# Score pairs put ahead of a block: an earlier third pair, fewer copied pairs, and two more blocks that begin ahead

## The chip, the core and the metric

The kernel runs on one core of a Trainium2 chip. The core has a matrix engine (TensorE, in the profile PE for matmuls and PEld for weight loads), three engines for elementwise work (VectorE = DVE, ScalarE = ACT, GpSimd = POOL), SyncE (SP), which issues most transfers, and 16 DMA engines. Every engine takes its own instructions in order and waits on semaphores for the others. Matmuls write to PSUM banks, from which VectorE and ScalarE read. The metric is the time of one execution on the device in microseconds; the median over the runs is compared.

## The reference

One block of a transformer, batch 1, 2048 tokens of 512 features, float32:

```python
x = A_x
xn = _layernorm(x, axis=-1)
s = _A_ref(xn, A_wqkv, A_wo)                      # softmax attention, 32 heads of 16, then @ wo
g = _silu(_B_ref(xn, B_w_gate, B_w_up, B_w_down)) # (silu(xn@w_gate) * (xn@w_up)) @ w_down, 1792 wide
return x + s * g
```

Attention is over all 2048 x 2048 pairs of every head, with a softmax scale of 16^-0.5.

## The kernel before

**Prologue** (the first exponential of the attention starts at 157.0 us): the layer norm, the transposes of the normalised tokens, and the projections to queries, keys and values, in four token blocks of 512. Each block has twelve tiles of output. A table `COPIES` says behind which of these tiles ScalarE copies pieces of the transposed tokens into `fx`, from which the feed-forward network reads later (16 pieces, 1.05 us each). In the same stretch ScalarE casts the transposed tokens of the next block into `xt` (L649), VectorE makes the residual of that cast (L652), and TensorE needs both at the next block's first tile. Projected tiles land in four PSUM buffers `ps`.

**Attention** then runs in 32 units (8 groups of 4 heads x 4 query blocks of 512), each over 16 key tiles of 128. A unit is cut into three blocks of 4 to 6 key tiles, which gives 96 blocks, numbered 0 to 95 by `now`. In a block of n key tiles there are 2n *pairs*: a pair is the scores of one key tile for two heads, two matmuls that use the upper and the lower half of the array's rows, 128 x 1024 numbers in all. A pair is turned to probabilities in one of two ways:

- *direct* (event D): both matmuls go into one of the two score tiles (two banks each), and ScalarE exponentiates straight from there into a pair buffer `pr` (L948). The two tiles alternate, so a pair's matmuls wait until the exponential of the pair two before it is done;
- *copied* (events A and B): the two halves go one after the other through one spare bank (`acc1`, in the order below `acc_81`), VectorE copies each to the pair buffer (L1005 and L1011), and ScalarE exponentiates it in place at the block's end (L1019).

Between these, TensorE works on the other branch: event F is one *product step*, two matmuls into `bankx` and `banky`, of the feed-forward network (L187) or, in the last nine blocks, of the output projection (L378). These D, A, B and F make up the block's *mixed part*. Behind it come the *values* (L407): the products of probabilities and values for the block's key tiles, four column tiles of the array at once, eight matmul records for each key tile, accumulated in `acc0`. There are 12 pair buffers.

What sets the order is a planner, `events(n, f)`: for a block of n key tiles and f product steps it decides how many pairs are copied, gives every D, A and B a mark on an abstract time line on which a product step and a direct pair are one unit, and fills the rest with F. The first two D are at marks 0 and 1, the next at 7, then one every `gap` units.

**The tail.** From block 87 (`early`) on, the product steps come from the output projection, and some blocks *begin ahead*: `run` leaves the last key tile's values of the block before, first scores two pairs of the next block (`begin`), and then does those last values. The exponentials of these two pairs can so run while TensorE ends the values. Before the change this holds for blocks 87, 88 and 89. The blocks from 87 have (n, f) = (6, 18), (5, 12), (5, 12), (6, 24), (6, 24), (4, 12), (4, 12), (6, 24), (6, 24).

The output projection splits each group of products in two halves, between which the two banks change row halves: before the second half TensorE waits for two one-element copies on VectorE, `turned_over` (L382), and behind the second VectorE takes the result from the banks (`closing`: L200 into `facc`, L361 with the gate). In block 87 this turn lies within the mixed part, after 9 of 18 steps; in 88 and 92 it falls at the block's end, since each has one half of a group. VectorE's other work (`chores`: transposes of finished units L418 and L443, residuals of the projection's operands L327, L453 and L1017) is put between the copies where the planner sees room, and the closing reads wait until the last copy of the block has been issued. GpSimd adds the result to x and stores it (L362, L363).

Of the kernel before, what the change touches and what calls it, by code (L numbers as in the profile page):

```python
# [21 lines left out]
D = 512  # L22
# [5 lines left out]
NT = TB // P  # L28
# [14 lines left out]
PROBS = 12  # L43
EPS = 1e-5
TURNS = (0, 0, 0, 0, 0, 2, 4, 6, 8, 10, 13, 16, 16)
COPIES = ((0, 0, 0, 1, 1, 1, 1, 0, 0, 0, 1, 1), (1, 1, 0, 0, 1, 1, 1, 1, 2, 2, 0, 0))
QSLOT = (0, 1, 0)
KSLOT = (0, 0, 1)

# [2 lines left out]
def tile_block(ctx: ExitStack, tc: tile.TileContext, x, wqkv, wo, w_gate, w_up, w_down, out):  # L52
# [87 lines left out]
    def tidy(room=None):  # L140
        while chores and (room is None or chores[0][0] <= room):
            cost, work = chores.pop(0)
            work()
            if room is not None:
                room -= cost
# [19 lines left out]
    def catch_up():  # L165
        while after:
            after.pop(0)()
# [30 lines left out]
    def close():  # L198
        while closing:
            closing.pop(0)()  # L200
# [136 lines left out]
    def out_steps():  # L337
        if now == early:
            for c in range(DT - 1):
                load_out(0, c)  # L340
        if now == early + 1:
            for c in range(DT - 1):
                load_out(1, c)
            for t in range(NT):
                load_gates(t)
        if now == early + 2:
            for c in range(DT - 1):
                load_out(2, c)
        if now == opened[units - 1] + 1:
            load_gate()  # L350

    def out_splits():
        for b, c in {early: ((0, 0), (0, 1), (0, 2)), early + 2: ((1, 0), (1, 1)), early + 3: ((1, 2),),
                     early + 5: ((2, 0), (2, 1)), early + 6: ((2, 2),)}.get(now, ()):
            split_out(b, c)
        if now == len(blocks) - 1:
            for j in range(EARLY):
                gate_rest(j)
# [109 lines left out]
    now = -1  # L468

    def fill(n):  # L470
        nonlocal given
        while n > 0 and queue:
            next(queue[0][0])
            queue[0][1] -= 1
            if not queue[0][1]:
                queue.pop(0)
            n -= 1
            given += 1
# [7 lines left out]
    early = len(sizes)  # L486
# [16 lines left out]
            blocks.append((u, kt, n))  # L503
            kt += n

    def events(n, f):
        length = 2 * n + f
        need = 2 * n - max(2, (10 * length + 46) // 40)
        fit = (10 * length + 55) // 112
        copied = max(0, min(need, fit)) if now else 0  # L510
        direct = 2 * n - copied
        gap = max(4, min(5, (length - 8) / max(1, direct - 2)))
        marks = [(0, "D"), (1, "D")] + [(7 + gap * i, "D") for i in range(direct - 2)]
        marks += [(2.2 + max(5.6, min(8, (length - 5) / (2 * copied))) * i, "AB"[i % 2]) for i in range(2 * copied)]
        marks.sort(key=lambda mark: mark[0] - 0.6 * (mark[1] == "D"))
        out = []
        at = left = 0
        for t, kind in marks:
            while left < f - (kind != "D") and at < t:
                out.append((at, "F"))  # L520
                left += 1
                at += 1
            out.append((at, kind))
            at += 1 if kind == "D" else 0.5
        return direct, out + [(at + i, "F") for i in range(f - left)]

    with ExitStack() as pro:
# [119 lines left out]
        def split_x(b, t, av, between=None):  # L647
            hi, lo = (xt[b % 2][j][:, :, t * P:(t + 1) * P] for j in range(2))
            nc.scalar.copy(hi, av)  # L649
            if between:  # L650
                between()
            dve.tensor_sub(lo, av, hi.bitcast(F32))  # L652
# [119 lines left out]
        def copy_fx(i):  # L772
            i, w = divmod(i, 2)
            i, u = divmod(i, 2)
            j, h = divmod(i, 2)
            dst = fx[halves[h], j].rearrange("p (c u) t -> u p c t", u=2)[u]
            nc.scalar.copy(dst[:, 2 * w:2 * w + 2], xt[0][j][halves[u], 2 * w:2 * w + 2])

        copied = list(range(16))
# [11 lines left out]
        for b in range(NB):  # L791
# [3 lines left out]
            for n, (make, i) in enumerate(slots):  # L795
# [27 lines left out]
                if b == 0 and n == 2:  # L823
                    split_x(0, 0, xf)
                for _ in range(COPIES[b][n] if b < 2 else 0):
                    copy_fx(copied.pop(0))
# [108 lines left out]
    now = 0  # L935
# [3 lines left out]
    def scores(u, bank, kt, j, h):  # L939
        k, kc = kst[(u // NB * NB + kt // CT) % RING], kt % CT  # L940
        r = slice(h * HALF, h * HALF + NROW)
        mm(bank, k[r, j, kc * P:(kc + 1) * P], qst[u % 2][r, j], start=True, stop=True)  # L942

    def scored(u, slot, kt, j):
        for h in order():
            scores(u, score[slot][:, h], kt, j, h)
        pr = ppool.tile([P, 2, TB], F32, tag="pr", name="pr")
        act(pr, score[slot], AF.Exp, scale=0.25)  # L948
        return pr

    begun = {}

    def begin(u, first, n):
        for j in range(2):
            begun[first, j] = scored(u, j, first, j)

    def run(u, first, n):
        nonlocal lower
        f = sizes.pop(0) if sizes else 0
        direct, todo = events(n, f)  # L960
        if now == 0:
            for _ in range(4):
                todo.insert(0, todo.pop(max(i for i, (_, e) in enumerate(todo) if e == "F")))
        if now >= early and f != pair // 2:
            behind = [i for i, (_, e) in enumerate(todo) if e == "F"][f // 2]
            near = min((i for i, (_, e) in enumerate(todo) if e == "D"), key=lambda i: abs(i - behind))
            todo.insert(behind - (near < behind), todo.pop(near))
        pairs = [(kt, j) for kt in range(first, first + n) for j in range(2)]
        straight, copies = pairs[:direct], pairs[direct:]
        probs, waiting, turned_in = {}, [], []  # L970

        def unit_end():
            while ends:
                ends.pop(0)()
            out_steps()

        done = len(begun)
        if done:
            probs.update(begun)
            begun.clear()  # L980
            todo = [i for i in todo if i not in ((0, "D"), (1, "D"))]
            unit_end()
        copying = [t + 1.5 for t, e in todo if e in "AB"]
        final = max(at for at, (_, e) in enumerate(todo) if e == "F")
        free = 0
        for at, (t, e) in enumerate(todo):
            if at == final and not copying:
                tidy()
            if e == "F":
                fill(1)  # L990
            elif e == "D":
                probs[straight[done]] = scored(u, done % 2, *straight[done])
                done += 1
                if done == 2:
                    unit_end()
            elif e == "A":
                if now > early and not turned_in:
                    turned_in.append(now)
                    out_splits()
                kt, j = copies.pop(0)  # L1000
                waiting.append((kt, j))
                scores(u, spare_bank, kt, j, 0)
                lower = True
                probs[kt, j] = ppool.tile([P, 2, TB], F32, tag="pr", name="pr")
                dve.tensor_copy(probs[kt, j][:, 0], spare_bank)  # L1005
                free = copying.pop(0) + 3
            else:
                kt, j = waiting[-1]
                scores(u, spare_bank, kt, j, 1)
                lower = False  # L1010
                dve.tensor_copy(probs[kt, j][:, 1], spare_bank)  # L1011
                free = copying.pop(0) + 3
            if not copying:
                close()
            while chores and at < final and (not copying or max(free, t) + chores[0][0] <= copying[0] + 0.5):
                free = max(free, t) + chores[0][0]
                chores.pop(0)[1]()  # L1017
        for kt, j in waiting:
            act(probs[kt, j], probs[kt, j], AF.Exp, scale=0.25)  # L1019
        tidy()  # L1020
        if not turned_in:
            out_splits()
            tidy()
        catch_up()
        kts = range(first, first + n)
        if early <= now + 1 < early + NT - 1:
            values(u, kts[:-1], probs)
            begin(*blocks[now + 1])
            values(u, kts[-1:], probs)
        else:  # L1030
            values(u, kts, probs)
# [104 lines left out]
```

## Time and profile before

| what | value |
|---|---|
| median of 3 runs (lowest to highest) | 1399.99 us (1399.34 to 1401.33) |
| profiled execution: time, span | 1399.14 us, 1397.4 us |
| TensorE clock granted in the profile | 1.0 |
| ScalarE exponentials from scores (L948) | 857, 1032 ns mean |
| ScalarE exponentials of copied pairs (L1019) | 167, 1080 ns mean |
| VectorE copies of half pairs (L1005, L1011) | 167 each, 692 and 691 ns mean |

A row of a timeline gives the start in us from the span's start, the length in us (from the first start to the last end where rows are merged), engine, line, operation, output<-inputs and shapes, how many were merged, and in brackets the idle time before it with what ended it. A row of the chain of waits gives the start, the time that the chain spent there, and engine, tile and line; it is followed back from the last instruction, and TensorE's marks in it lie 0.07 us behind the starts of the timeline. Matmuls overlap, two row halves and one after the other, so starts and not lengths show TensorE's pace.

### The profile page before, as it was taken

The numbers are of one execution on the slowest core, as the hardware profiler recorded it, in microseconds if no ns is written. First come the engines' busy times: TensorE is split into PE (matmuls) and PEld (weight loads), VectorE is DVE, ScalarE is ACT, GpSimd is POOL, SyncE is SP. The second block draws the span as 40 slices with busy tenths as digits, with TensorE's granted clock in tenths as the row PEclk, the third lists the DMA queues.
The fourth block names the chain that finished last, engine by engine and source line by source line (L and its number), as shares of the span: only waits on it lengthen the run. The fifth ranks groups of instructions, "written<-read, shape, count | busy, mean of one in ns | idle before, by whom it ended". The sixth has DMA issues, their size and how long they took to land.

```text
span 1397.4 us, 27647 instructions
## 1 busy us (share of the span) xinstructions
PE 1388.9 (99%) x11193; PEld 848.9 (61%) x11193; DVE 763.1 (55%) x1299; ACT 1087.9 (78%) x1245; POOL 73.9 (5%) x92
## 2 busy tenths in 40 slices
PE   9999999999999999999999999999999999999998
PEld 7777755655665665566556556655655665565555
DVE  6674555455645653556456635554565446556454
ACT  6753678877888877787888778778877887888885
POOL 4200200000000000000000000000000000000222
PEclk9999999999999999999999999999999999999999
DMA  7778741043634411254514303356224113225323
GB/s 228 270 244 266 181 102 43 13 116 84 133 85 118 118 43 36 54 134 92 139 51 110 94 13 73 76 145 145 63 73 112 35 47 73 66 88 163 99 74 142
DMA packets 126953, 148.13 MB, mean 106 GB/s; under 512 B 12524, under 2 KB 79340, under 8 KB 126052
## 3 DMA queue, kind: packets, MB, share of 16 engines
q1 hardware_dynamic: 121620, 125.79, 35.3%
q0 software_dynamic: 4912, 20.12, 3.8%
q8 instruction: 89, 1.46, 0.5%
q14 instruction: 44, 0.36, 0.1%
q10 hardware_dynamic: 288, 0.39, 0.1%
HBM read 106.68 MB, written 39.58 MB: 105 GB/s over the span
## 4 chain that ended last, share of the span: by engine, by line
PE 87%; ACT 1%; issue 0%; DVE 0%; DVEq 0%; ACTq 0%
PE acc L407 32%; PE bankx L187 23%; PE score L942 16%; PE banky L187 9%; PE acc L942 3%; PE bankx L378 1%; PE banky L378 1%; ACT pr L948 1%; PE acc L1073 0%; PE bankx L1073 0%; PE score L1073 0%; DVE pr L1005 0%; DVE y L1080 0%; DVE y L1086 0%; DVEq L1132 0%
## 5 line engine op out<-in xcount | busy, mean ns | idle before, releaser
L948 ACT ACTIVATE pr<-score 128x1024 f32<-128x1024 f32 x857 | 810.3, 1032 | 227.8 <-PE score L942 226.3
L407 PE MATMUL acc<-pr,vst 128*17 128x512 f32 x4096 | 459.7, 593 | 0.0
L942 PE MATMUL score<-qst,kst 50*128 50x512 f32 x1714 | 393.8, 413 | 1.5 <-ACT pr L948 1.4
L187 PE MATMUL bankx<-fx,guh 64*128 64x512 f32 x896 | 333.2, 393 | 0.1
L187 PE MATMUL banky<-fx,guh 64*128 64x512 f32 x896 | 324.6, 393 | 0.0
L407 PEld LDWEIGHTS acc<-pr,vst 128*17 128x17 f32 x4096 | 110.4, 97 | 291.6 <-issue 269.9
L942 PEld LDWEIGHTS score<-qst,kst 50*128 50x128 f32 x1714 | 174.6, 184 | 147.0 <-issue 73.1
L1005 DVE COPY pr<-acc 128x512 f32<-128x512 f32 x167 | 115.5, 692 | 191.6 <-PE acc L942 187.5
L187 PE MATMUL bankx<-wd,hh 64*128 64x512 f32 x672 | 199.9, 392 | 0.0
L187 PE MATMUL banky<-wd,hh 64*128 64x512 f32 x672 | 197.7, 393 | 0.0
L187 PEld LDWEIGHTS bankx<-fx,guh 64*128 64x128 f32 x896 | 166.4, 186 | 18.5 <-issue 0.9
L187 PE MATMUL banky<-fx,gul 64*128 64x512 f32 x448 | 175.5, 392 | 0.0
L187 PE MATMUL bankx<-fx,gul 64*128 64x512 f32 x448 | 175.2, 391 | 0.0
L1019 ACT ACTIVATE pr<-pr 128x1024 f32<-128x1024 f32 x167 | 171.2, 1080 | 0.0
L187 PEld LDWEIGHTS banky<-fx,guh 64*128 64x128 f32 x896 | 166.4, 186 | 5.1
L1011 DVE COPY pr<-acc 128x512 f32<-128x512 f32 x167 | 115.4, 691 | 74.3 <-PE acc L942 63.4
L240 DVE SCALAR_TENSOR_TENSOR ga<-th,bankx 128x512 f32<-128x512 f32 x56 | 38.5, 688 | 178.4 <-ACT th L239 178.4
L942 PE MATMUL acc<-qst,kst 50*128 50x512 f32 x334 | 134.2, 402 | 0.1
L187 PEld LDWEIGHTS bankx<-wd,hh 64*128 64x128 f32 x672 | 125.0, 186 | 12.9
L187 PEld LDWEIGHTS banky<-wd,hh 64*128 64x128 f32 x672 | 124.5, 186 | 3.3
L187 PEld LDWEIGHTS bankx<-fx,gul 64*128 64x128 f32 x448 | 83.6, 187 | 10.4
L187 PEld LDWEIGHTS banky<-fx,gul 64*128 64x128 f32 x448 | 83.5, 186 | 2.5
(184 smaller groups left out, 1298.2 us busy)
## 6 DMA issues: line engine op xcount, KB each, us to landing
gur<-in_B_w_gate_dram SPq DMA_DIRECT2D x56, 256.0 KB
gur<-in_B_w_up_dram SPq DMA_DIRECT2D x56, 256.0 KB
wdr<-in_B_w_down_dram SPq DMA_DIRECT2D x56, 256.0 KB
kst<-k_d SPq DMA_DIRECT2D x192, 64.0 KB
qst<-q_d SPq DMA_DIRECT2D x192, 64.0 KB
fx<-xt_d SPq DMA_DIRECT2D x24, 512.0 KB
q_d<-parts SPq DMA_DIRECT2D x16, 512.0 KB
k_d<-parts SPq DMA_DIRECT2D x16, 512.0 KB
```

The costliest lines, as they stand in the source:

```text
L187: mm(banks[i], lhs[halves[i]], rhs[halves[i]], start=start, stop=stop)
L240: dve.scalar_tensor_tensor(ga, th, 1.0, bankx, op0=ALU.add, op1=ALU.mult)
L378: mm(banks[k], lhs[b, c][a][halves[h], (j + k) * P:(j + k + 1) * P], fx[halves[h], w, c], start=swap == i == 0, stop=i == 3 * n - 1, skip_ ...
L407: mm(acc[0][h * 32:h * 32 + DH + 1], v[:, kt % CT, h * (DH + 1):(h + 1) * (DH + 1)], probs[kt, h // 2][:, h % 2], start=kt == 0, stop=kt = ...
L942: mm(bank, k[r, j, kc * P:(kc + 1) * P], qst[u % 2][r, j], start=True, stop=True)
L948: act(pr, score[slot], AF.Exp, scale=0.25)
L1005: dve.tensor_copy(probs[kt, j][:, 0], spare_bank)
L1011: dve.tensor_copy(probs[kt, j][:, 1], spare_bank)
L1019: act(probs[kt, j], probs[kt, j], AF.Exp, scale=0.25)
```

## The change

Three edits:

1. `events` is told how many pairs were put ahead (`ahead`, 0 or 2). With 2 it doesn't plan the first two D, counts the block as two units shorter, marks the third pair at 0.5 instead of 7 and the first half copy at 0.3 instead of 2.2, and copies n - 3 pairs. For n = 6 and n = 5 that is as many as before (3 and 2), for n = 4 it is 1 instead of 2. The line in `run` that took the first two D out afterwards goes.
2. The blocks that begin ahead are 87, 88, 89 and now also 92 and 93, the two blocks of 4 key tiles.
3. In the first prologue block, the `fx` copy that stood behind the eleventh tile goes behind the twelfth, beside the one there.

```diff
-COPIES = ((0, 0, 0, 1, 1, 1, 1, 0, 0, 0, 1, 1), (1, 1, 0, 0, 1, 1, 1, 1, 2, 2, 0, 0))
+COPIES = ((0, 0, 0, 1, 1, 1, 1, 0, 0, 0, 0, 2), (1, 1, 0, 0, 1, 1, 1, 1, 2, 2, 0, 0))
...
-    def events(n, f):
-        length = 2 * n + f
+    def events(n, f, ahead):
+        length = 2 * n - ahead + f
         need = 2 * n - max(2, (10 * length + 46) // 40)
         fit = (10 * length + 55) // 112
-        copied = max(0, min(need, fit)) if now else 0
+        copied = n - 3 if ahead else max(0, min(need, fit)) if now else 0
         direct = 2 * n - copied
         gap = max(4, min(5, (length - 8) / max(1, direct - 2)))
-        marks = [(0, "D"), (1, "D")] + [(7 + gap * i, "D") for i in range(direct - 2)]
-        marks += [(2.2 + max(5.6, min(8, (length - 5) / (2 * copied))) * i, "AB"[i % 2]) for i in range(2 * copied)]
+        marks = [] if ahead else [(0, "D"), (1, "D")]
+        marks += [((0.5 if ahead else 7) + gap * i, "D") for i in range(direct - 2)]
+        marks += [((0.3 if ahead else 2.2) + max(5.6, min(8, (length - 5) / (2 * copied))) * i, "AB"[i % 2]) for i in range(2 * copied)]
...
-        direct, todo = events(n, f)
+        direct, todo = events(n, f, len(begun))
...
-            todo = [i for i in todo if i not in ((0, "D"), (1, "D"))]
...
-        if early <= now + 1 < early + NT - 1:
+        if now + 1 - early in (0, 1, 2, 5, 6):
```

The number of pair buffers (12) stays. Lines between `events` and the removed line in `run` stand one lower in the changed kernel: L942 becomes L943, L948 becomes L949; L1005, L1011 and L1019 stay.

On VectorE, at the start of block 87, before (`acc_81` is the spare bank, `acc_80` holds the values of the unit that ended, `wor` and `fx` are the last output weights being split):

```order
L1017 CAST fx<-wor 128x512
L1005 COPY pr<-acc_81 128x512
L1017 TENSOR_TENSOR fx<-wor,fx 128x512
L1011 COPY pr<-acc_81 128x512
L418 STREAM_TRANSPOSE o<-acc_80 128x512
L382 COPY turned_over<-bankx 1x1
L382 COPY turned_over<-banky 1x1
L1005 COPY pr<-acc_81 128x512
L423 RECIPROCAL rl<-o 128x16
```

and after:

```order
L1017 CAST fx<-wor 128x512
L1005 COPY pr<-acc_81 128x512
L1011 COPY pr<-acc_81 128x512
L1017 TENSOR_TENSOR fx<-wor,fx 128x512
L1005 COPY pr<-acc_81 128x512
L418 STREAM_TRANSPOSE o<-acc_80 128x512
L382 COPY turned_over<-bankx 1x1
L382 COPY turned_over<-banky 1x1
L1011 COPY pr<-acc_81 128x512
L423 RECIPROCAL rl<-o 128x16
```

The third half copy has moved ahead of the transpose and the two `turned_over` copies.

On TensorE, where block 91's values end and block 92's mixed part starts, before (`score0` and `score1` are the two score tiles, `acc1_81` the spare bank, and `acc0_80` with `pr` the values):

```order
L407 MATMUL acc0_80<-pr_21302,vst0_550 17x512 x2
L407 MATMUL acc0_80<-pr_21209,vst0_550 17x512 x2
L407 MATMUL acc0_80<-pr_21250,vst0_550 17x512 x2
L942 MATMUL score0_8970<-qst0_557,kst1_553 128x512 x2
L942 MATMUL score1_8971<-qst0_557,kst1_553 128x512 x2
L378 MATMUL bankx_78<-fx_82,wd_8969 128x512
L378 MATMUL banky_79<-fx_82,wd_8969 128x512
L942 MATMUL acc1_81<-qst0_557,kst1_553 128x512
```

and after:

```order
L407 MATMUL acc0_80<-pr_21302,vst0_550 17x512 x2
L943 MATMUL score0_8970<-qst0_557,kst1_553 128x512 x2
L943 MATMUL score1_8971<-qst0_557,kst1_553 128x512 x2
L407 MATMUL acc0_80<-pr_21209,vst0_550 17x512 x2
L407 MATMUL acc0_80<-pr_21250,vst0_550 17x512 x2
L378 MATMUL bankx_78<-fx_82,wd_8969 128x512
L378 MATMUL banky_79<-fx_82,wd_8969 128x512
L943 MATMUL score0_8970<-qst0_557,kst1_553 128x512 x2
L943 MATMUL acc1_81<-qst0_557,kst1_553 128x512
```

The two first pairs now stand ahead of the last key tile's values, and the third pair directly behind the first product step; in blocks 87 to 89 it moves from behind the fifth step to the same place.

On ScalarE in the prologue, at the last two tiles of the first block, before:

```order
L777 COPY fx<-xt_161 64x2x512
L649 CAST xt_163<-acc_81 128x4x128
L745 ACTIVATE sq<-ps 128x512
L746 CAST parts<-ps 128x512
L777 COPY fx<-xt_161 64x2x512
```

and after, one line number lower in the file:

```order
L650 CAST xt_163<-acc_81 128x4x128
L746 ACTIVATE sq<-ps 128x512
L747 CAST parts<-ps 128x512
L778 COPY fx<-xt_161 64x2x512 x2
L746 ACTIVATE sq<-ps 128x512
```

The cast of the next block's tokens is now ahead of both copies. Transfers on SyncE and GpSimd stand in the same order as before.

## The prediction

> **What bounds the kernel now.** I read the page first, for the engine shares, then the chain of waits over the last blocks, then the timelines of the three engines there.
>
> ```profile
> PE 1388.9 (99%) x11193; PEld 848.9 (61%) x11193; DVE 763.1 (55%) x1299; ACT 1087.9 (78%) x1245; POOL 73.9 (5%) x92
> ```
>
> TensorE is the bound: 1388.9 us of a span of 1397.4. But a TensorE shown as busy can still be stretched by waits, so I measure the blocks against each other. In the chain of waits, each run of value products (L407) marks where a block's mixed part (scores, projection products, half copies) ends.
>
> ```profile
> 1235.34 0.67 PE score L942 x4
> ...
> 1242.87 4.42 PE acc L407 x40
> ...
> 1271.89 0.66 PE score L942 x4
> 1272.55 0.98 PE acc L407 x8
> 1273.54 0.43 PE bankx L378
> ...
> 1281.36 4.42 PE acc L407 x40
> 1285.78 0.67 PE score L942 x4
> 1286.44 0.98 PE acc L407 x8
> 1287.42 0.43 PE bankx L378
> ...
> 1293.77 3.56 PE acc L407 x32
> ...
> 1298.98 0.42 PE banky L378
> ...
> 1305.34 4.42 PE acc L407 x40
> ...
> 1332.89 5.28 PE acc L407 x48
> 1338.17 0.66 PE score L942 x4
> ...
> 1343.28 4.13 PE acc L407 x32
> 1347.40 0.66 PE score L942 x4
> ...
> 1352.82 4.02 PE acc L407 x32
> 1356.84 0.66 PE score L942 x3
> ```
>
> A product step is two matmuls, a direct pair two, a half copy one. The first stretch is a block with 21 steps, 8 pairs and 4 half copies: 62 matmuls from 1235.34 to 1242.87, 7.53 us, or 121 ns each. That is my clean price. Block 87 (18 steps, 7 pairs, 6 halves, 56 matmuls) should take 6.80 by it and takes 7.82 (1273.54 to 1281.36): 1.0 of waits. Blocks 88 and 89 (12 steps, 6 pairs, 4 halves, 40 matmuls) should take 4.86 and take 6.35 and 6.36: 1.5 each. Blocks 92 and 93 (40 matmuls) take 5.11 and 5.42, 0.25 and 0.56 over, and their 32 value matmuls take 4.13 and 4.02 where block 88's first 32 take 3.56: 0.57 and 0.46. Together 5.8 us. With the small prologue wait below, this is all that the change can win: 0.4%.
>
> **Blocks 88 and 89: the third pair.** Who is waited for there, first on ScalarE, then on TensorE:
>
> ```profile
> 1286.31 1.94 ACT L948 ACTIVATE pr<-score 128x1024 f32<-128x1024 f32 x2 [0.89 <-PE score L942]
> 1289.36 5.70 ACT L948 ACTIVATE pr<-score 128x1024 f32<-128x1024 f32 x6 [1.11 <-PE score L942]
> 1294.92 2.03 ACT L1019 ACTIVATE pr<-pr 128x1024 f32<-128x1024 f32 x2
> ...
> 1300.90 5.71 ACT L948 ACTIVATE pr<-score 128x1024 f32<-128x1024 f32 x6 [1.09 <-PE score L942]
> ...
> 1288.61 0.40 PE L942 MATMUL score<-qst,kst 50*128 50x512 f32 x1
> ...
> 1292.36 0.50 PE L942 MATMUL score<-qst,kst 50*128 50x512 f32 x2 [0.28 <-ACT pr L948]
> 1293.28 0.50 PE L942 MATMUL score<-qst,kst 50*128 50x512 f32 x2 [0.41 <-ACT pr L948]
> ```
>
> ScalarE does the two pairs put ahead from 1286.31 to 1288.25, then idles 1.11, because the third pair's scores start at 1288.61, behind five product steps, and take 0.75 to reach it. Then it runs without a gap, 0.95 a pair, and at the end TensorE waits for it: the last two pairs find their banks still being read. The change puts the third pair behind one product step. That step costs 0.43 here (the chain at 1287.42), so the scores start at about 1287.78 and ScalarE at 1288.5: the idle time falls from 1.11 to some 0.25. The six exponentials move forward 0.9, and so does the last score pair, which ends the mixed part. The part then takes 5.45, still above 4.86, so TensorE's own work doesn't take the gain back. **-0.9 each**, -1.8. Ends: 0 (if something else paces the pairs) and -1.5 (all waits go). I take the value by ScalarE's row, since the last wait names it.
>
> **Block 87: the same move meets VectorE's queue.** Its rows, with TensorE's first half copy and its restart after the bank turn:
>
> ```profile
> 1273.81 0.39 PE L942 MATMUL acc<-qst,kst 50*128 50x512 f32 x1
> 1276.91 0.49 PE L378 MATMUL bankx<-fx,part 64*128 64x512 f32 x1
> ...
> 1274.24 0.69 DVE L1005 COPY pr<-acc 128x512 f32<-128x512 f32 x1 [1.88 <-PE acc L942]
> 1274.85 0.68 DVE L1017 TENSOR_TENSOR fx<-wor,fx 128x512 fp32r<-128x512 f32 x1
> 1275.52 0.69 DVE L1011 COPY pr<-acc 128x512 f32<-128x512 f32 x1
> 1276.12 0.71 DVE L418 STREAM_TRANSPOSE o<-acc 128x512 f32<-128x512 f32 x1
> 1276.76 0.10 DVE L382 COPY turned_over<-bankx 1x1 f32<-1x1 f32 x1
> 1276.85 0.67 DVE L1005 COPY pr<-acc 128x512 f32<-128x512 f32 x1
> ```
>
> TensorE may start the second half of the products only when the two `turned_over` copies are done (1276.76; it restarts at 1276.91). Now only two half copies stand ahead of them on VectorE. The new order puts a third there, with the transpose behind it. Step by step: the extra score pair (two matmuls, 0.23) moves the first half copy's matmul from 1273.81 to 1274.04. From matmul to copy takes 0.43, the copy 0.69, the next matmul follows 0.05 after it, so copies start at 1274.47 and 1275.64. The residual (L1017) follows at 1276.25; the third copy's matmul, freed at 1276.38, is copied at 1276.86; transpose 1277.47, turn 1278.11, TensorE at about 1278.26. That is 1.35 later than now, with two more matmuls already done (29 ahead of the turn, not 27: 0.24). Behind the turn 27 matmuls are left instead of 29: 3.27 clean. The last half copy waits there for its predecessor, as the present block does: its 29 matmuls from 1276.91 take 4.38, 0.87 more than clean. With none of that, the values start at 1281.53, 0.2 later than now (1281.29 on the timeline, 0.07 before the chain's mark); with all of it 1282.40, 1.1 later. **+0.6**, between them. The lower end, if no stall forms, is -1.0. `facc` copies move behind a transpose, a cast and a subtraction on VectorE, about 1.8 us; they read banks that block 88 wants only after 40 value matmuls and a pair put ahead (6.06 us), so they cost nothing. If that cover fell short, the excess would stand before block 88.
>
> **Blocks 91 to 93: two more pairs put ahead, two fewer copied pairs.** A pair of pairs ahead costs a round trip: four scores 0.66 and eight values 0.98 (block 88's rows), against 0.48 and 0.88 inside a long run: 0.28, twice. [...] New, without waits: values of 91 4.42 + 0.66 + 0.98 = 6.06; mixed part of 92 with 12 steps, 5 pairs, 2 halves, 36 matmuls: 4.36; its values 2.67 + 0.66 + 0.98 = 4.31; block 93 4.36 + 3.56. Sum 22.65. Now, from 1332.89 to 1356.84: 23.95. So -1.3 at best. If the mixed parts keep their waits of 0.25 and 0.56, -0.5. The value waits (0.57, 0.46) should go, for they are waits for the last copied pairs:
>
> ```profile
> 1344.31 2.00 ACT L1019 ACTIVATE pr<-pr 128x1024 f32<-128x1024 f32 x2
> 1353.73 2.02 ACT L1019 ACTIVATE pr<-pr 128x1024 f32<-128x1024 f32 x2
> ```
>
> One of each two goes, and ScalarE starts each block earlier, during the values before. VectorE sheds four copies of 0.69, beside other work. The 12 pair buffers hold: when block 91's last key tile is left, ten of its twelve pairs are used up. **-0.8**; ends -1.3 and +0.5 (two round trips paid, mixed parts as long as now with four matmuls fewer).
>
> **Prologue.** One `fx` copy goes behind a cast:
>
> ```profile
> 42.86 1.05 ACT L777 CAST fx<-xt 64x1024 fp32r<-64x1024 f32 x1
> 43.94 0.59 ACT L649 CAST xt<-acc 128x512 fp32r<-128x512 f32 x1
> 44.09 0.63 PE L694 MATMUL ps<-xt,wh 128*128 128x512 f32 x2
> 44.79 1.01 PE L694 MATMUL ps<-xt,wh 128*128 128x512 f32 x2
> ```
>
> Two matmuls there span 1.01 where two others span 0.63. TensorE waits 0.3 to 0.4 for VectorE's split of that cast. The cast comes 1.08 sooner, so the wait goes: **-0.3** (0 to -0.4). The copy now follows another; four `ps` buffers cover ScalarE's later start on the next tile, and without that cover 0.3 would come back.
>
> **Sum.** -0.3 - 1.8 + 0.6 - 0.8 = **-2.3 us**. The profiled execution took 1399.14 (span 1397.4 and 1.7 around it): 1396.8. The median of the runs, 1399.99, lies 0.85 above it; against that I forecast **1397.7 us**, 0.16% less. About 0.2% (2.8 us, below 1397.2 or above 1402.8) is what a measurement of this kernel can tell from no change.
>
> **Rivals.**
> *No stall at the turn.* If VectorE's queue lets the turn through in time, block 87 gains 1.0 instead of losing 0.6: -3.9, 1396.1. For it: the estimate is a chain of eight steps of 0.05 to 0.7. Against it: VectorE does its work in order, and each step has a row.
> *The last part gives nothing.* The waits in 92 and 93 stay and eat the -0.8: -1.5, 1398.5. For it: only part of them names ScalarE, and two round trips are certain. Against it: copied pairs halve.
> *Half copies pace TensorE.* One turn of the spare bank takes 1.28 (1274.24 to 1275.52). If all six in block 87, with residual, transpose and turn (1.45), run one behind the other from 1274.47, the mixed part takes 10.1, +2.3; in 88 and 89 four turns with 1.0 of start make 6.1, close to 6.35, so no gain: -0.3 + 2.3 - 0.8 = +1.2, 1401.2. It decides once a turn exceeds 1.3 us in 88. Against it: in 88 TensorE's last rows wait for ScalarE.
>
> **Chances.** My forecast 0.52, with -1.2 to -3.3 as its own range; no stall 0.17; nothing in the last part 0.20; half copies 0.08; anything else 0.03. Faster by over 0.2%: the no-stall case and a third of the forecast, 0.34. Slower by over 0.2%: 0.03. Within: 0.63. The range runs from the no-stall case with the full -1.3 (1395.6) to just past unchanged (1400.2), between the empty last part and the half copies.
>
> **What would show it.** Right: ScalarE's gap after two exponentials in 88 and 89 near 0.25 and mixed parts near 5.45; in 87 a TensorE hole near 1.3 ahead of the turn; 91 to 93 in about 23.1; no hole at 44.79. Wrong: mixed parts of 88 or 89 above 6, a block 87 under 7.2, or blocks 90, 94 and 95, which nothing touches, off by over 0.3.

## The result and the profile after

The changed kernel takes 1397.77 us (median of 22 runs, 1397.23 to 1398.67) beside 1399.52 for the kernel before (22 runs, 1398.86 to 1401.33): 1.75 us less, a ratio of 0.9986 with a 95% interval of 0.9980 to 0.9992. That is 0.13% faster: the interval leaves out 1, so the gain is clear of the scatter of these runs, but it is inside the 0.2% within which the prediction counts a kernel as unchanged. The profiled execution took 1397.74, with a span of 1396.0 (1397.4 before).

The engine shares on the page of the changed kernel hardly moved:

```profile
PE 1388.3 (99%) x11193; PEld 849.1 (61%) x11193; DVE 756.9 (54%) x1295; ACT 1087.4 (78%) x1245; POOL 74.3 (5%) x92
```

VectorE lost four copies, TensorE has the same 11193 matmuls. What changed is the pace of single blocks, in the chain of waits of the changed kernel (start, time spent there, engine, tile and line):

```profile
1273.61 0.43 PE bankx L378
...
1278.50 0.49 PE bankx L378
...
1282.49 4.42 PE acc L407 x40
...
1288.55 0.43 PE bankx L378
...
1294.08 3.56 PE acc L407 x32
...
1299.29 0.43 PE banky L378
...
1304.81 4.42 PE acc L407 x40
...
1332.37 4.42 PE acc L407 x40
1336.78 0.67 PE score L943 x4
1337.45 0.98 PE acc L407 x8
1338.43 0.43 PE bankx L378
...
1343.00 2.70 PE acc L407 x24
1345.70 0.66 PE score L943 x4
1346.36 0.98 PE acc L407 x8
1347.34 0.43 PE banky L378
...
1351.92 3.56 PE acc L407 x32
1355.47 0.66 PE score L943 x4
```

Read against the same marks of before:

| stretch | before | after | difference | forecast |
|---|---|---|---|---|
| block 87, mixed part (1273.61 to 1282.49) | 7.82 | 8.88 | +1.06 | +0.6 |
| block 88, mixed part (1288.55 to 1294.08) | 6.35 | 5.53 | -0.82 | -0.9 |
| block 89, mixed part (1299.29 to 1304.81) | 6.36 | 5.52 | -0.84 | -0.9 |
| values of 91 to block 94 (1332.37 to 1355.47) | 23.95 | 23.10 | -0.85 | -0.8 |
| prologue, TensorE's 120th to 240th matmul | 25.35 | 24.98 | -0.37 | -0.3 |
| sum | | | -1.82 | -2.3 |

The sum agrees with the measured -1.75 within the scatter of the runs. Blocks 90 and 91 (8.97 and 8.90), 94 and 95 (8.92 and 8.88) and the stretch of matmuls behind them (7.46) are unchanged to 0.02.

In blocks 88 and 89, ScalarE's timeline (in brackets the idle time before a group and its releaser):

```profile
1287.43 3.84 ACT L949 ACTIVATE pr<-score 128x1024 f32<-128x1024 f32 x4 [1.94 <-PE score L943]
1291.59 3.77 ACT L949 ACTIVATE pr<-score 128x1024 f32<-128x1024 f32 x4 [0.32 <-PE score L943]
...
1298.17 3.85 ACT L949 ACTIVATE pr<-score 128x1024 f32<-128x1024 f32 x4 [0.93 <-PE score L943]
1302.32 3.77 ACT L949 ACTIVATE pr<-score 128x1024 f32<-128x1024 f32 x4 [0.30 <-PE score L943]
```

The gap of 1.11 behind the second exponential is gone; a smaller one, 0.32, comes two pairs later.

In block 87, VectorE's timeline and TensorE's restart:

```profile
1274.55 0.69 DVE L1005 COPY pr<-acc 128x512 f32<-128x512 f32 x1 [2.11 <-PE acc L943]
1275.82 0.69 DVE L1011 COPY pr<-acc 128x512 f32<-128x512 f32 x1 [0.59 <-PE acc L943]
1276.43 0.68 DVE L1017 TENSOR_TENSOR fx<-wor,fx 128x512 fp32r<-128x512 f32 x1
1277.11 0.69 DVE L1005 COPY pr<-acc 128x512 f32<-128x512 f32 x1
1277.71 0.70 DVE L418 STREAM_TRANSPOSE o<-acc 128x512 f32<-128x512 f32 x1
1278.34 0.10 DVE L382 COPY turned_over<-bankx 1x1 f32<-1x1 f32 x1
...
1279.73 0.69 DVE L1011 COPY pr<-acc 128x512 f32<-128x512 f32 x1 [1.21 <-PE acc L943]
...
1281.00 0.69 DVE L1005 COPY pr<-acc 128x512 f32<-128x512 f32 x1
1282.29 0.69 DVE L1011 COPY pr<-acc 128x512 f32<-128x512 f32 x1 [0.59 <-PE acc L943]
...
1278.50 0.49 PE L378 MATMUL bankx<-fx,part 64*128 64x512 f32 x1 [0.96 <-DVE turned_over L382]
...
1282.41 1.05 PE L407 MATMUL acc<-pr,vst 128*17 128x512 f32 x8
```

The turn comes at 1278.34 instead of 1276.76, and TensorE idles 0.96 for it. Counted from the start of its last matmul ahead of the turn (1277.15) to its restart (1278.50), the hole is 1.35; the texts below use *hole* for this distance between starts and *idle time* for the number in brackets. The 1.58 are made of three pieces. The first half copy starts 0.31 later (1274.55 for 1274.24). The other two lie between the second half copy and the transpose, which stand 1.89 apart now (1275.82 to 1277.71) and stood 0.60 apart before (1275.52 to 1276.12): the third half copy, and the residual L1017. The residual lay before in the gap between the first two half copies (1274.85); now it follows the second and leaves that gap of 0.59 empty.

### The profile page after: what moved, and what is told of

It reads as the page before. It is cut to its first block, busy times and chain, and to the rows that moved or that the text cites. A ratio compares the mean times of both kernels' runs of the same rounds, so it can differ in the third digit from the quotient of the medians.

```text
span 1396.0 us, 27644 instructions
## 1 busy us (share of the span) xinstructions
PE 1388.3 (99%) x11193; PEld 849.1 (61%) x11193; DVE 756.9 (54%) x1295; ACT 1087.4 (78%) x1245; POOL 74.3 (5%) x92
## 4 chain that ended last, share of the span: by engine, by line
PE 88%; DVE 0%; ACT 0%; issue 0%; DVEq 0%
PE acc L407 32%; PE bankx L187 22%; PE score L943 17%; PE banky L187 10%; PE acc L943 3%; PE bankx L378 2%; PE banky L378 1%; ACT pr L949 0%; PE acc L1073 0%; PE bankx L1073 0%; PE score L1073 0%; DVE pr L1011 0%; DVE pr L1005 0%; DVE y L1080 0%; DVE o L418 0%
## 5 line engine op out<-in xcount | busy, mean ns | idle before, releaser
L949 ACT ACTIVATE pr<-score 128x1024 f32<-128x1024 f32 x859 | 812.4, 1032 | 226.6 <-PE score L943 225.0
L943 PE MATMUL score<-qst,kst 50*128 50x512 f32 x1718 | 394.4, 413 | 0.1
L943 PEld LDWEIGHTS score<-qst,kst 50*128 50x128 f32 x1718 | 175.8, 184 | 143.4 <-issue 68.9
L1005 DVE COPY pr<-acc 128x512 f32<-128x512 f32 x165 | 114.0, 691 | 193.6 <-PE acc L943 188.6
L1019 ACT ACTIVATE pr<-pr 128x1024 f32<-128x1024 f32 x165 | 169.0, 1078 | 0.0
L1011 DVE COPY pr<-acc 128x512 f32<-128x512 f32 x165 | 114.0, 691 | 75.5 <-PE acc L943 62.4
L943 PE MATMUL acc<-qst,kst 50*128 50x512 f32 x330 | 132.7, 402 | 0.1
```

## The experiments

The theory by the prediction: block 87 loses by VectorE's queue ahead of the turn; 88 and 89 win by the earlier third pair; 92 and 93 win by all their edits. The rivals: 87 loses by something else, half copies pace the parts, or the blocks of 4 key tiles give nothing. The diffs are against the changed kernel where nothing else is said.

**Block 87 planned as before, the rest as changed.**

```diff
-        direct, todo = events(n, f, len(begun))
+        direct, todo = events(n, f, len(begun) if now != early else 0)
...
             begun.clear()
+            if now == early:
+                todo = [i for i in todo if i not in ((0, "D"), (1, "D"))]
```

> The changed kernel, with block 87 alone planned as in the kernel before (third pair at mark 7); blocks 88, 89, 92, 93 and the prologue keep the change. Theory (the new order in 87 puts a third half copy and the transpose ahead of the turn on VectorE, and TensorE waits for the turn): block 87's mixed part goes from 8.88 us back to 7.8, nothing else moves, and the kernel gains 1.0 to 1.1 us on the changed one, about 2.8 on the one before. Rival (the loss in 87 pays for the gain in 88, because pairs come late there when 87 is short): 88 goes back above 6.0 and the total stays within 0.4 us of the changed kernel.

Measured: 1396.56 us (11 runs, 1396.27 to 1396.83) beside 1399.33, ratio 0.9977 (0.9968 to 0.9986). The chain of waits of this kernel, blocks 87 and 88:

```profile
1273.51 0.42 PE bankx L378
...
1281.35 4.42 PE acc L407 x40
...
1287.42 0.42 PE bankx L378
...
1292.96 3.56 PE acc L407 x32
```

Block 87 is back at 7.84 and 88 keeps its 5.54. So the early third pair is worth its gain in 88 and 89 and costs 1.04 in 87 alone. This kernel is the fastest of all here: 2.77 below the one before, where the change won 1.75.

**A third half copy done twice in block 87.** The same PSUM half is copied to the same place once more, so that VectorE has one copy more ahead of the turn.

```diff
                 dve.tensor_copy(probs[kt, j][:, 0], spare_bank)
+                if now == early and len(waiting) == 2:
+                    dve.tensor_copy(probs[kt, j][:, 0], spare_bank)
```

> The changed kernel with the third half copy of block 87 done twice on VectorE, one 0.69 us copy more ahead of the transpose and the turn. Theory (VectorE's queue sets the turn): the hole ahead of the turn grows from 1.35 by 0.6 to about 1.95, and block 87's mixed part from 8.88 to about 9.5. Rival (the turn waits for TensorE's own work or for ScalarE): the mixed part stays within 0.1 us of 8.88.

Measured: 1399.88 us (one run), and 11.08 for the mixed part of block 87 (1273.32 to 1284.40 in the chain) where 9.5 was expected. The hole grew as the theory says, TensorE's idle time from 0.96 to 1.68:

```profile
1278.92 0.59 PE L378 MATMUL bankx<-fx,part 64*128 64x512 f32 x1 [1.68 <-DVE turned_over L382]
```

The other 1.5 have another cause. Stretches of this kernel (first two numbers the window and its length; busy time and instructions of TensorE, its loads, VectorE, ScalarE and GpSimd; then the granted clock, DMA share and GB/s):

```profile
1273.25:1276.85 3.60, 3.60 (x33) 2.89 (x29) 2.02 (x4) 3.35 (x4) 0.00 (x0) 1.00 0.97 311
1278.92:1279.17 0.25, 0.25 (x2) 0.25 (x4) 0.01 (x1) 0.00 (x0) 0.00 (x0) 1.00 1.02 393
1279.17:1282.58 3.41, 3.41 (x18) 3.41 (x18) 1.27 (x3) 1.02 (x1) 0.00 (x0) 0.50 1.01 341
1282.58:1284.43 1.85, 1.77 (x16) 0.97 (x17) 0.91 (x2) 1.83 (x3) 0.00 (x0) 1.00 0.50 185
```

Behind the hole the granted clock stood at 0.50 for 3.41 us. From the restart to the start of the 18th matmul behind it TensorE takes 3.50 here (1278.92 to 1282.42) and 2.02 in the changed kernel (1278.50 to 1280.52), for the same matmuls. The part is 2.20 longer than the change's: 0.72 by the hole and 1.48 behind it. Two runs followed from this: the same kernel again, and one with a smaller copy.

**Half of such a copy.**

```diff
+                if now == early and len(waiting) == 2:
+                    dve.tensor_copy(probs[kt, j][:, 0, :256], spare_bank[:, :256])
```

> The changed kernel with half of a copy more (128x256) ahead of block 87's turn on VectorE. The whole copy made the hole 0.72 longer, and behind it TensorE's granted clock was 0.5 for 3.4 us, which cost 1.5 more. If the clock falls with the length of the hole: a hole of about 1.35 + 0.4, with an idle time of 1.3 to 1.4 us against 0.97 in the changed kernel and 1.68 with the whole copy, either keeps the clock (block 87 at 9.3, kernel +0.4) or loses it (10.7, kernel +1.8); that gives the side on which 1.35 us lies. If the fall was chance, the clock stays at 1.0 here.

Measured: 1398.18 us (10 runs, 1397.92 to 1398.95) beside 1399.57, ratio 0.9991 (0.9981 to 1.0000).

```profile
1278.82 0.49 PE L378 MATMUL bankx<-fx,part 64*128 64x512 f32 x1 [1.43 <-DVE turned_over L382]
```

The idle time is 1.43 and the clock stays at 1.00; block 87 takes 9.33 (1273.47 to 1282.80), 0.45 above the change, for 0.47 more of idle time. In both sizes, what is put ahead of the turn on VectorE comes back as idle time of about its own length (0.72 for the copy of 0.69, 0.47 for the half of 0.42).

**The doubled copy again, in ten runs.**

> The kernel with one whole copy more ahead of block 87's turn once more, timed. If the fall of TensorE's clock belongs to the hole of 2.07 us (1.68 idle): it shows again in the profile, block 87 takes 11.1, and the kernel is 2.0 to 2.3 us slower than the changed one, as the single time of 1399.88 was. If it was chance: block 87 takes 9.6, and the kernel is 0.7 slower than the changed one.

Measured: 1399.84 us (1398.24 to 1400.60) beside 1399.70, ratio 0.9996 (0.9987 to 1.0006). In its profile the idle time is 1.69, block 87 takes 10.66, and the clock falls again, later:

```profile
1279.02:1280.58 1.56, 1.56 (x13) 1.56 (x15) 0.34 (x2) 0.44 (x1) 0.00 (x0) 1.00 0.91 297
1280.58:1284.00 3.42, 3.42 (x17) 2.55 (x14) 1.96 (x5) 2.59 (x4) 0.00 (x0) 0.50 0.86 318
```

The spans of the ten runs lie in two groups: 1396.5, 1396.5 and 1396.6, and seven from 1397.6 to 1398.7. Three lie about 0.7 above the middle of the changed kernel's spans (1395.8), which is the longer hole alone; the seven add 1.1 to 2.2. That the seven are those with a fallen clock fits: the mean granted clock on record is 0.998 for six of the seven, and 0.999 for the three and for the seventh (1398.7), which it leaves open. Only the profiled run shows the fall directly. Against its own kernel before, this one is 0.14 slower where the change was 1.75 faster: 1.9 slower than the changed one, close to the 2.0 to 2.3 expected for a fall that belongs to the hole, and far from the 0.7 expected if it were chance.

**The third half copy behind the turn.** The two later copied pairs of block 87 are marked 3.5 units later.

```diff
+        if ahead and f == 18:
+            marks = [(m + (3.5 if k in "AB" and m > 8 else 0), k) for m, k in marks]
         marks.sort(key=lambda mark: mark[0] - 0.6 * (mark[1] == "D"))
```

> The changed kernel with the second and third copied pair of block 87 planned 3.5 units later, so that the third half copy stands behind the turn; third pair early as in the change. Theory (the turn waits for what stands ahead of it on VectorE, one copy of 0.6 less): the hole falls from 1.35 to 0.5 to 0.7; but the four half copies left need 1.28 each behind the turn, so the block ends no earlier, at 8.7 to 9.2. Rival (the hole is made by the early pairs on TensorE itself): the hole stays above 1.2.

Measured: 1398.39 us (one run). The turn on VectorE and two rows of TensorE that waited in this kernel (its lines stand two lower from L943 on):

```profile
1277.64 0.10 DVE L382 COPY turned_over<-bankx 1x1 f32<-1x1 f32 x1
...
1277.86 0.50 PE L378 MATMUL banky<-fx,part 64*128 64x512 f32 x1 [0.45 <-DVE turned_over L382]
...
1282.10 0.49 PE L945 MATMUL acc<-qst,kst 50*128 50x512 f32 x1 [0.78 <-DVE pr L1007]
```

TensorE's idle time shrinks from 0.96 to 0.45 and the hole from 1.35 to 0.85 (1277.01 to 1277.86), less than expected but far below the rival's 1.2. Yet the part takes 9.23 (1273.60 to 1282.83), just above the range expected and longer than the change's 8.88: now four half copies stand behind the turn, and TensorE waits 0.78 for the last of them. The hole doesn't vanish because the turn is still at 1277.64, 0.88 later than before: of the pieces above, the first half copy's later start (0.28 here, at 1274.52) and the residual outside the gap (0.60) stay. So, with the early third pair, the third half copy costs in either place; in the order of before the part takes 7.82.

**The third pair behind three product steps in 88 and 89.**

```diff
-        marks += [((0.5 if ahead else 7) + gap * i, "D") for i in range(direct - 2)]
+        marks += [((3 if ahead and n == 5 else 0.5 if ahead else 7) + gap * i, "D") for i in range(direct - 2)]
```

> The changed kernel with the third pair of blocks 88 and 89 behind three product steps instead of one (five in the kernel before). Theory (its place alone sets ScalarE's gap and so the end of the mixed part): two steps of 0.23 later than changed, mixed parts of 5.9 to 6.0, between 5.54 and 6.35. Rival (the half copies or the shorter planned length made the gain): 5.5 to 5.6 as in the changed kernel.

Measured: 1399.39 us (one run); mixed parts of 5.89 and 5.90, and ScalarE's gap behind the second exponential (the last row ends where the view's window does, at 1306):

```profile
1290.36 5.72 ACT L949 ACTIVATE pr<-score 128x1024 f32<-128x1024 f32 x6 [0.62 <-PE score L943]
...
1301.46 4.81 ACT L949 ACTIVATE pr<-score 128x1024 f32<-128x1024 f32 x5 [0.63 <-PE score L943]
```

Gap and part move together: 1.11 and 6.35, 0.62 and 5.89, none and 5.53 (there with the later gap of 0.32). The half copies and the planned length are those of the changed kernel, so the rival is out: the place of the third pair, with the direct pairs behind it (their marks move along), is what sets these blocks.

**Blocks 92 and 93, taken apart.** Four kernels, each with some of the edits there. The first has no pairs ahead in 92 and 93, which puts all back there that hangs on them:

```diff
-        if now + 1 - early in (0, 1, 2, 5, 6):
+        if now + 1 - early in (0, 1, 2):
```

> The changed kernel without pairs ahead in blocks 92 and 93, which are then planned as before (two copied pairs each). Theory: from the values of block 91 to the start of block 94 it takes 23.95 us again, not 23.10, and the kernel is 0.85 us slower than the changed one. Rival (these blocks gave nothing and the gain lies elsewhere): the same as the changed kernel within 0.2 us.

The second has pairs ahead and the early third pair, but two copied pairs:

```diff
-        copied = n - 3 if ahead else max(0, min(need, fit)) if now else 0
+        copied = max(2, n - 3) if ahead else max(0, min(need, fit)) if now else 0
```

> The changed kernel with two copied pairs in blocks 92 and 93 instead of one (pairs still put ahead). If the fewer copies are what gains there: the stretch from block 91's values to block 94 goes from 23.10 us towards 23.95, by ScalarE's second exponential in place (0.95) at each end. If putting pairs ahead is what gains: the values stay at their clean 3.56, the mixed parts grow by at most 0.4 each, and the stretch is 23.1 to 23.9.

The third is the kernel before, with pairs ahead in 92 and 93 and nothing else:

```diff
-        if early <= now + 1 < early + NT - 1:
+        if now + 1 - early in (0, 1, 2, 5, 6):
```

> The kernel before with pairs put ahead in 92 and 93 too, and nothing else: third pair at mark 7, two copied pairs, as its planner has it. If putting ahead alone gains: the stretch from block 91's values to block 94 is below 23.7 instead of 23.95. If it needs the early third pair and the fewer copies: 23.9 to 24.5, since two round trips cost 0.28 each and a late third pair leaves ScalarE idle as in block 88 of that kernel.

The fourth has no pairs ahead in 92 and 93, but one copied pair:

```diff
-        copied = n - 3 if ahead else max(0, min(need, fit)) if now else 0
+        copied = n - 3 if ahead or n == 4 and now > early else max(0, min(need, fit)) if now else 0
...
-        if now + 1 - early in (0, 1, 2, 5, 6):
+        if now + 1 - early in (0, 1, 2):
```

> The changed kernel without pairs ahead in 92 and 93, but with one copied pair there instead of two. If fewer copies alone make the gain of 0.85 us: the stretch from block 91's values to block 94 is 23.1 to 23.4. If the copies had been there to relieve ScalarE, and only pairs put ahead let it do without: the mixed parts become longer than the 5.1 and 5.4 of the kernel before, and the stretch is 24.2 to 24.7.

| kernel | values of 91 to block 94 | mixed 92, 93 | time, ratio |
|---|---|---|---|
| before | 23.95 | 5.11, 5.42 | 1399.52 |
| changed | 23.10 | 4.57, 4.58 | 1397.77, 0.9986 |
| no pairs ahead | 23.96 | 5.12, 5.41 | 1398.40, 0.9992 (0.9983 to 1.0001) |
| two copied pairs | 24.18 | 5.11, 5.10 | 1398.81, 0.9994 (0.9984 to 1.0003) |
| pairs ahead alone | 24.01 | 4.64, 4.94 | 1399.62, 1.0001 (0.9991 to 1.0011) |
| one copied pair alone | 23.99 | 5.79, 5.81 | 1400.40 (one run) |

Without pairs ahead the two blocks are as they were before, and the kernel wins 0.93 where the change wins 1.75: the difference, 0.82, is about the stretch's 0.86. The other three have a reason in their rows. With pairs ahead alone, ScalarE idles behind the second exponential as in 88, and in 93 two copied pairs still follow at the end:

```profile
1340.65 3.88 ACT L948 ACTIVATE pr<-score 128x1024 f32<-128x1024 f32 x4 [1.09 <-PE score L942]
...
1349.92 3.77 ACT L948 ACTIVATE pr<-score 128x1024 f32<-128x1024 f32 x4 [1.36 <-PE acc L942]
1353.55 2.02 ACT L1019 ACTIVATE pr<-pr 128x1024 f32<-128x1024 f32 x2
```

Against the changed kernel this costs little in 92 (4.64 for 4.57). Nearly all of the loss of 0.91 is in 93: 0.36 in its mixed part, and 0.47 in its values, which take 4.03 where 3.56 is clean.

With one copied pair alone, the value waits go (3.56 twice), but seven exponentials run back to back in each block and set the length of the mixed part:

```profile
1338.03 6.54 ACT L949 ACTIVATE pr<-score 128x1024 f32<-128x1024 f32 x7 [2.79 <-PE score L943]
```

I had expected longer mixed parts, which came, and a stretch of 24.2 to 24.7, which did not. Its one time is no verdict on this: VectorE's last work starts 5.9 us before the end of its span, in the changed kernel 4.0, so 1.9 of it lie behind that work.

With two copied pairs the values are clean, as expected, but the mixed parts are 0.5 longer each than the changed kernel's, not 0.4 at most, and 24.18 lies outside both expected ranges. The half copies pace block 92, VectorE's rows:

```profile
1339.47 0.69 DVE L1005 COPY pr<-acc 128x512 f32<-128x512 f32 x1 [5.98 <-PE acc L943]
...
1340.74 0.69 DVE L1011 COPY pr<-acc 128x512 f32<-128x512 f32 x1 [0.25 <-PE acc L943]
...
1342.09 0.69 DVE L1005 COPY pr<-acc 128x512 f32<-128x512 f32 x1
...
1343.37 0.69 DVE L1011 COPY pr<-acc 128x512 f32<-128x512 f32 x1 [0.25 <-PE bankx L378]
```

Four starts 1.27 to 1.35 apart, the turn of the spare bank: with 36 matmuls (4.36 clean) the part takes 5.11, so here the rival of the half copies is true. None of the three partial sets wins anything: pairs ahead alone 24.01, pairs ahead with the early third pair 24.18, one copied pair alone 23.99, beside 23.95. All three together win 0.85. As I read the rows, pairs ahead give ScalarE its start, the early third pair keeps it going, and the copied pair that goes takes two turns out of a short part and an exponential out of its end. No kernel has pairs ahead and one copied pair with the third pair left late, so that the early third pair is needed here too is argued, not shown.

**The prologue's copy alone,** the kernel before with the new table:

```diff
-COPIES = ((0, 0, 0, 1, 1, 1, 1, 0, 0, 0, 1, 1), (1, 1, 0, 0, 1, 1, 1, 1, 2, 2, 0, 0))
+COPIES = ((0, 0, 0, 1, 1, 1, 1, 0, 0, 0, 0, 2), (1, 1, 0, 0, 1, 1, 1, 1, 2, 2, 0, 0))
```

> The kernel before with the moved prologue copy alone. Theory: the hole at 44.79 (start to start 0.51) shrinks to the usual 0.23, nothing else moves: 0.3 us faster. Rival (the prologue wait is made up for later): the same time within 0.1 us.

Measured: 1399.26 us beside 1399.33, ratio 1.0000 (0.9991 to 1.0009). TensorE's rows of this kernel there:

```profile
44.79 0.40 PE L694 MATMUL ps<-xt,wl 128*128 128x512 f32 x1
45.02 0.64 PE L694 MATMUL ps<-xt,wh 128*128 128x512 f32 x2
```

The changed kernel has the same starts. Two matmuls that spanned 1.01 span 0.64, and the stretch of 120 matmuls is 0.37 shorter. Whether the whole kernel is, these runs can't tell: their interval is 1.3 us to either side, and their median is only 0.07 lower.

Two other readings point opposite ways. For a gain: in the changed kernel and four of its variants (block 87 as before, no pairs ahead, two copied pairs, half a copy) the time won is larger than the four stretches of the table from block 87 on add up to, by 0.30 to 0.42 (1.75 against 1.45 in the changed kernel). In the kernel with pairs ahead alone, which keeps the old table, the two agree within 0.01. Against it: TensorE's 1000th matmul, behind the prologue's projections, starts at 189.32 in the profile of before and between 189.15 and 189.74 in the profiles with the new table. They are behind already at the 40th matmul, ahead of the moved copy (11.59 to 12.17, and 11.52 before).

## Why the prediction was right, and where it was not

The forecast was 1397.7 and "within 0.2%"; measured were 1397.77 and -0.13%. That the two numbers agree to 0.1 is partly luck: the forecast was -2.3 on a median of 1399.99; the change won 1.75, 0.55 less, on a median that turned out 0.47 lower. Of the 0.55, 0.46 is block 87.

- **What bounds.** TensorE stays at 99%, and all that moved lay in waits inside the blocks. Right.
- **88 and 89, -0.9 each.** -0.82 and -0.84. The cause is settled by the kernel with the third pair behind three steps, which lands between the two. The detail was off: no gap of 0.25 came behind the second exponential; one of 0.32 and 0.30 came two pairs later, before a score pair. What holds that pair back wasn't tried by itself. "Still above 4.86" held: 5.53 and 5.52.
- **87, +0.6.** This is the term that was mis-sized: it measured +1.06, by the chain's marks. The mechanism was right, as the kernel with block 87 undone and the two sizes of extra copy show, and the hole of 1.35 fits the "near 1.3" forecast. The working had two ends, 0.2 later and 1.1 later, and took the middle; the result lies at the upper end, for two reasons of about 0.2 each. First, the waits behind the restart: the working knew 0.87 of them from the present block and counted half, 0.43. They measured 0.64: 27 matmuls take 3.91 where 3.27 would be clean (1278.50 to 1282.41), with three half copies in a row, copied at 1279.73, 1281.00 and 1282.29. Second, the restart came 0.17 later than in the working (1278.50 for 1278.26, in a part that began 0.07 later). Of that, 0.10 is the second half copy, which the working set 1.17 behind the first and which came 1.27 behind, the same turn of 1.28 that the prediction used elsewhere. The rest is the third, which came 0.68 behind the residual instead of 0.61. So the upper end was met by both together, and not because all waits came.
- **91 to 93, -0.8 ("about 23.1").** 23.10. The value waits went as forecast; the mixed parts are 0.2 above clean each. That pairs ahead alone, or one copied pair fewer alone, would win nothing was not foreseen.
- **Prologue, -0.3.** The hole is gone and the stretch 0.37 shorter in the profiles; its worth in the total stays open.
- **Rivals.** *No stall at the turn* didn't happen. The kernel with block 87 as before shows what is left without one, 1396.56; the further 1.0 that this rival claimed in 87 no run reached. *The last part gives nothing* is false as a whole, but true for each of the three partial sets. *Half copies pace TensorE* is false for the changed 88 and 89 as a gain of zero, true in 87 behind the turn, and true in block 92 with two copied pairs.

## What to carry to other kernels

Before a step is moved ahead on one engine, look at what waits behind it on the others' queues: here one 0.69 us copy delayed a 0.1 us copy that TensorE needed, and a residual that slipped out of the gap between two copies cost about as much again. A rule that helps some blocks need not hold in the block with another critical wait; undoing it there alone won 1.0 us more than the change. Edits that win nothing one at a time can win together when one removes what stops the other, so a missing gain of one edit is no verdict on the set.

## What the runs showed of the hardware

In block 87 a short hole in TensorE's work cost more than itself: with the copy done twice the hole was 0.72 longer than in the changed kernel, and the part 2.20. With an idle time of 1.68 and 1.69 us the granted clock fell to 0.50 behind it, for 3.41 and 3.42 us, after 0.25 us of full clock in one profile and 1.56 in the other; with 1.43 (profile at 1.00, ten runs within 0.5 us of span) and 0.96 it stayed at 1.00. In this place, then, both profiles with 1.68 us or more have the fall, those with 1.43 or less don't, and nothing between the two was run. From the start of the idle time to the fall it is 1.93 us in the one profile (1277.24 to 1279.17) and 3.26 in the other (1277.32 to 1280.58). Of the ten runs with the copy done twice, three have a span 0.7 to 0.8 above the middle of the changed kernel's, the other seven 1.8 to 2.9. Why the fall came at another distance in each profile, and why three runs lack the longer time, no run here shows.
